# Attention and a feed-forward block on one core: weight loads moved to ScalarE's queue, the value scale taken through DRAM, the first batch's wide jobs moved behind the first hidden layer, half of a weight's low parts moved to VectorE

## The chip, the cores and the metric

The kernel runs on one core of a Trainium2 chip. The metric is the time of one execution in microseconds (us), the median of the runs taken. The core has a matrix engine (TensorE, PE in the profile, its weight loads PEld), VectorE (DVE), ScalarE (ACT), GpSimd (POOL) and SyncE (SP). Each runs its own instructions in a fixed order. DMAs are issued by SP and by ACT, in the order in which they stand among that engine's instructions; an engine that must wait before it issues a DMA keeps everything behind it waiting too. All DMAs are carried by the same 16 DMA engines.

## The reference

```python
# attention: batch 8, heads 8, 576 positions, head size 64; q, k, v, s are float32
scores = scale * np.matmul(q, k.transpose(0, 1, 3, 2))
cum = np.cumsum(np.maximum(s, 0.0), axis=-1)
bias = -(cum[:, :, :, None] - cum[:, :, None, :])
scores = np.where(causal, -1000000000.0, scores + np.minimum(bias, 0.0))
attn = softmax(scores)                       # row maximum taken off, eps 1e-9 in the sum
x = (attn @ v) as 4608 tokens x 512
# feed-forward: w_in 512 x 2048 and w_out 2048 x 512 are float64
h = x @ w_in
g = np.where(h >= 1, h, np.where(h <= -1, 0.0, (h + 1) ** 2 / 4))
out = (g @ w_out).astype(np.float32)
```

## The kernel before

Every product of the feed-forward block is made of three 16-bit products: each operand is split into a high and a low half (both float16), and high x high, low x high and high x low are added in PSUM. So weights, `x` and `g` are all held as pairs of halves.

**Weights.** `w_in` (w1 in the code) and `w_out` (w2) arrive as 64-bit numbers in 16 chunks each, 512 KB a chunk. `Weights.load` (L190) loads one into a raw buffer; there are four raw buffers for each weight, so that a later load waits until an earlier chunk has been read out. `decode` rebuilds float32 from the two words: a copy on ACT (L199), a shift on DVE (L200), one more ACT pass for every second chunk (L212), one or two combining passes on DVE (L213, or L215 and L216), and a matmul with ones (L204) that sums a group for its bound. `scale` turns a group's sums into a power-of-two factor (w1 has four groups, w2 two). `split` then makes the halves: the high one on ACT (L229); the low one either on DVE in one instruction (L237) or, for the chunks in the table `POOL_LO`, on POOL (L235), which for w2 needs one more ACT pass first (L234). w2's loads begin only when `a_in`, the largest bound of w1, is known (L623, L185), and so do the scales that every hidden activation needs.

**Attention** goes through 64 jobs: a batch has four head pairs, each with a narrow half (the first 320 queries, three query tiles) and a wide half (the last 256 queries over all 576 keys, two tiles). All four narrow jobs of a batch come first, then its four wide ones. A job loads q and k (L328 for the first eight jobs, L344 later), makes scores (L411; later L416 and L417), takes mask and row minimum on DVE (L422), exponentials on ACT (L433), row sums and their reciprocal on DVE (L449, L450), splits the weights into halves `pb` on POOL and DVE (L454 to L460), transposes them by DMA into `pt` (L461), multiplies by the transposed values `vt` (L479) and leaves `x` (L490, L491). `att_slot` deals a job out in eight slots.

**Value scale.** For each batch the largest magnitude of v over all 128 partitions is needed in every partition (`msc`, in `batch_scales_v`). `column_max` turns the column of 128 maxima into a row by a PE transpose (L97) and takes its maximum on DVE (L99); `spread` converts it (L105), multiplies it by ones on PE (L107) and copies the resulting column out of PSUM (L108).

**Feed-forward.** `ffn_h` makes one of 16 tiles of the hidden layer from `x` (12 matmuls, L534), ACT and DVE turn it into g (L546, L549, L550), ACT and POOL split it (L560, L561). `ffn_y` multiplies g by w2 (L573). Each batch has a narrow and a wide half here too.

**What sets the order.** The program is written as one stream, and a scheduler puts each instruction in its engine's order by priority and by an estimate of time; `tc.high_priority` moves what it encloses ahead. At the start the stream holds the first narrow jobs beside the 16 chunks of w1. Then a loop over `j` begins: in the first 16 steps it holds the hidden layer of the first narrow half, in the next 16 the products with w2 of that half; beside them stand w2's decoding and splitting (`w2_tasks`, two tasks a step, so 16 steps) and slots of attention, 40 in these 32 steps:

```python
for _ in range(1 + (j % 4 == 3 if j < 2 * NFT else j % 8 == 3 and j < 6 * NFT)):
    att_slot(t // 8, t % 8)
    t += 1
```

SP's queue carries s, q, k, v, all weight chunks, the transposes by DMA and the cumulated sums; ACT's carries outputs and two small loads a job.

## Time and profile before

| | |
|---|---|
| median of 3 runs | 1113.92 us (1113.88 to 1118.03) |
| the profiled execution's own time | 1117.59 us |
| span of its profile | 1115.8 us |
| busy: PE, PEld | 1013.1 us (91%), 777.3 us (70%) |
| busy: DVE, ACT, POOL | 843.6 us (76%), 731.0 us (66%), 637.1 us (57%) |
| DMA packets | 340925, 155.09 MB |
| transfers on SP's queue (q1), on ACT's (q10) | 143.68 MB, 9.84 MB |

The span runs from the first to the last instruction of the program; the execution's own time holds a little more, 1.8 us here. Busy time is an average over stages: in the profile's 40 slices PE is at 3 to 8 tenths in the first seven and at 8 or 9 from then on, so the start of the program and its long middle have to be read apart.

### The profile page before, as it was taken

To read this page: it belongs to the slowest core of one execution; us is meant where nothing else is said; L and a number is where in the kernel's file an instruction comes from. 1 tells how busy PE (TensorE), PEld (TensorE's weight loads), DVE (VectorE), ACT (ScalarE), POOL (GpSimd) and SP (SyncE) were. 2 spreads that over 40 slices of the span, in tenths; PEclk is the share of its full clock that TensorE was granted. 3 is DMA by queue.
4 is the path that set the end of the run, shared out by engine and by line. 5 is a ranking of instruction groups with operands and counts; after the bars stand their busy time and mean duration, and the time that the engine had idled before them with its cause. 6 is when DMAs were issued, how large, how long until landed. Compare 5 with 4: busy or idle time off the path is not lost.

```text
span 1115.8 us, 24709 instructions
## 1 busy us (share of the span) xinstructions
PE 1013.1 (91%) x8495; PEld 777.3 (70%) x8496; DVE 843.6 (76%) x2327; ACT 731.0 (66%) x1711; POOL 637.1 (57%) x846
## 2 busy tenths in 40 slices
PE   3558788899999999899999999899988999999998
PEld 1224456687777877787777877687767877787787
DVE  6877895787777877787877887787777888887533
ACT  4856787677576765777576765677576756776432
POOL 3555667666456664566566655556467665666422
PEclk9967889899999999999999999999999999999999
DMA  6986864776387663878377764668379663776300
GB/s 222 213 190 178 177 143 103 157 153 153 83 166 164 150 139 84 190 156 152 83 160 163 147 136 84 169 147 165 68 159 181 145 145 80 162 155 126 67 25 20
DMA packets 340925, 155.09 MB, mean 139 GB/s; under 512 B 290984, under 2 KB 322572, under 8 KB 340800
## 3 DMA queue, kind: packets, MB, share of 16 engines
q1 hardware_dynamic: 331200, 143.68, 60.2%
q10 hardware_dynamic: 9600, 9.84, 2.7%
q8 instruction: 67, 1.10, 0.4%
q14 instruction: 58, 0.48, 0.1%
HBM read 72.28 MB, written 9.88 MB: 74 GB/s over the span
## 4 chain that ended last, share of the span: by engine, by line
PE 58%; DMA 12%; DVE 11%; POOL 8%; issue 6%; ACT 4%; SPq 1%; ACTq 0%; DVEq 0%; POOLq 0%
PE h L534 25%; PE y L573 23%; DMA pt<-pb 5%; PE px L479 4%; PE s L416 3%; PE s L417 3%; DMA wir<-in_moe_w_in_dram 2%; POOL pb L457 2%; POOL pb L454 2%; DMA vt<-vb 2%; DVE pb L460 2%; DVE PS L422 1%; POOL g L561 1%; DMA wor<-in_moe_w_out_dram 1%; DVE h L549 1%
## 5 line engine op out<-in xcount | busy, mean ns | idle before, releaser
L534 PE MATMUL h<-x,WI 128*128 128x256 f16 (+1 forms) x3072 | 462.8, 292 | 8.0 <-DVE u L550 6.2
L573 PE MATMUL y<-g,WO 128*128 128x256 f16 (+1 forms) x3072 | 451.0, 288 | 9.7 <-POOL g L561 7.3
L534 PEld LDWEIGHTS <-WI 128*128 128x128 f16 x3072 | 290.3, 100 | 106.0 <-issue 21.4
L573 PEld LDWEIGHTS <-WO 128*128 128x128 f16 x3072 | 287.8, 98 | 97.0 <-issue 18.6
L561 POOL TENSOR_TENSOR g<-u,g 128x320 f16<-128x320 f32 (+1 forms) x256 | 208.6, 815 | 175.8 <-ACT g L560 175.5
L433 ACT ACTIVATE PS<-PS,mn 64x64 f32<-64x64 f32 (+4 forms) x320 | 178.8, 559 | 131.4 <-DVE mn L422 114.3
L546 ACT ACTIVATE u<-h,ub,us 128x320 f32<-128x320 f32 (+1 forms) x256 | 148.8, 582 | 116.1 <-PE h L534 100.9
L454 POOL TENSOR_SCALAR pb<-PS,rs 64x128 f16<-64x128 f32 (+4 forms) x160 | 101.0, 631 | 207.1 <-DVE rs L450 136.1
L549 DVE SCALAR_TENSOR_TENSOR h<-h,ws,u 128x320 f32<-128x320 f32 (+1 forms) x256 | 132.3, 518 | 107.8 <-ACT u L546 106.5
L457 POOL TENSOR_TENSOR pb<-PS,pb 64x128 f16<-64x128 f32 (+4 forms) x160 | 168.0, 1050 | 11.5
L460 DVE SCALAR_TENSOR_TENSOR pb<-PS,rs,pb 64x128 f16<-64x128 f32 (+4 forms) x160 | 135.1, 845 | 49.6 <-POOL pb L454 49.0
L422 DVE CUSTOM_DVE_ANT_0 PS<-s,mask 64x64 f32<-64x64 f32 (+4 forms) x320 | 133.3, 419 | 26.3 <-PE s L417 23.4
L550 DVE SCALAR_TENSOR_TENSOR u<-u,r,h 128x320 f32<-128x320 f32 (+1 forms) x256 | 130.0, 508 | 6.6
L416 PE MATMUL s<-K,Q 128*64 128x64 f32 (+1 forms) x336 | 126.3, 378 | 6.2 <-DVE mn L422 2.6
L455 ACT ACTIVATE PS<-PS,rs 64x64 f32<-64x64 f32 (+4 forms) x160 | 88.9, 559 | 49.2 <-DVE rs L450 49.1
L560 ACT CAST g<-u 128x320 f16<-128x320 f32 (+1 forms) x256 | 107.9, 422 | 13.5 <-DVE u L550 13.4
L417 PE MATMUL s<-K,Q 68*64 68x64 f32 (+1 forms) x336 | 102.8, 309 | 7.2 <-POOL K L367 4.3
L479 PEld LDWEIGHTS <-vt 128*64 128x64 f16 x1536 | 73.5, 114 | 49.2 <-issue 37.2
L479 PE MATMUL px<-pt,vt 128*64 128x256 f16 (+3 forms) x1536 | 83.4, 259 | 23.7 <-DMA pt<-pb 20.9
L456 POOL TENSOR_SCALAR pb<-PS 64x128 f16<-64x128 f32 (+4 forms) x160 | 90.5, 566 | 21.0 <-ACT PS L455 19.0
L416 PEld LDWEIGHTS s<-K,Q 128*64 128x64 f32 (+1 forms) x336 | 61.5, 183 | 17.1 <-DVE mn L422 3.2
L417 PEld LDWEIGHTS s<-K,Q 68*64 68x64 f32 (+1 forms) x336 | 61.9, 185 | 9.5 <-POOL K L367 4.4
(108 smaller groups left out, 930.3 us busy)
## 6 DMA issues: line engine op xcount, KB each, us to landing
rk<-in_k_dram SPq DMA_DIRECT2D x56, 288.0 KB
v<-in_v_dram SPq DMA_DIRECT2D x32, 288.0 KB
rq<-in_q_dram SPq DMA_DIRECT2D x56, 160.0 KB
rk<-in_k_dram SPq DMA_DIRECT2D x56, 160.0 KB
wir<-in_moe_w_in_dram SPq DMA_DIRECT2D x16, 512.0 KB
wor<-in_moe_w_out_dram SPq DMA_DIRECT2D x16, 512.0 KB
rq<-in_q_dram SPq DMA_DIRECT2D x56, 128.0 KB
out_dram<-o ACTq DMA_DIRECT2D x32, 160.0 KB
```

The source lines that it names most:

```text
L416: T.matmul(sc[:R, :c1 - c0], Q1[:, hd, qo:qo + R], K1[:, hd, c0:c1], start=True, stop=False)
L417: T.matmul(sc[:R, :c1 - c0], Q2[:KC, hd, qo:qo + R], K2[:KC, hd, c0:c1], start=False, stop=True)
L422: ttr[0] = V.tensor_tensor_reduce(out=Pt[:R, c0:c1], in0=sc[:R, :c1 - c0], in1=mask[:R, mo:mo + c1 - c0], scale=-0.125 if j < F32_JOBS els ...
L433: A.activation(Pt[:R, :W], Pt[:R, :W], AF.Exp, bias=m2[:R], scale=-1.0, accum_out=sums[n, i][:R, hd:hd + 1])
L457: G.tensor_tensor(los[1], pw, his[1], ALU.subtract)
L460: V.scalar_tensor_tensor(los[0], pv, rs[:R, :1], his[0], ALU.mult, ALU.subtract)
L479: T.matmul(px[hd * D:(hd + 1) * D, lo:N], VT[:, vl * NB + j, hd * D:(hd + 1) * D], PT[:, 4 * j + 2 * hd + pl, lo:], start=(m == 0), stop=( ...
L534: T.matmul(h[:, :N], WI[4 * kt + ft // 4][:, wl, ft % 4 * P:(ft % 4 + 1) * P], x[:, kt, xl], start=(n == 0), stop=(n == 3 * NKT - 1),)
L546: first = A.activation(u, h[:, :N], AF.Relu, bias=ubi[b], scale=usc[b][:, fg:fg + 1]).ins
L549: V.scalar_tensor_tensor(h[:, :N], h[:, :N], wsc[b][:, fg:fg + 1], u, ALU.mult, ALU.max)
L561: G.tensor_tensor(g[:, 1], u, g[:, 0], ALU.subtract)
L573: T.matmul(ys[b, hf, m][:, :N], WO[8 * (m // 2) + ft // 2][:, wl, c0:c0 + P], g[:, gl], start=(ft == 0 and n == 0), stop=(ft == NFT - 1 an ...
```

## The change

Five things change.

1. The chunks of both weights are issued by ACT (`WQ = nc.scalar`) in place of SP. The first three loads stand ahead of the first q and k in the program, and s, the cumulated sum, these three loads and the first job's q and k are given a higher priority.
2. The value scale goes through DRAM: the column of 128 maxima is written to a DRAM tensor `md`, read back broadcast to all partitions as `ma` (both DMAs on SP), and DVE takes the maximum of 128 numbers in each partition. `column_max`, `spread` and the identity matrix with its two POOL instructions go.
3. The 40 slots of attention that stood beside the first 32 steps all stand in the second 16 steps (two and three a step).
4. `POOL_LO['wo']` holds every second chunk in place of all: eight of w2's low halves are made on DVE by one instruction each, and their eight extra ACT passes go.
5. Some memsets at the start stand in another order.

```diff
-POOL_LO = {'wi': (8, 12, 13, 14, 15), 'wo': range(16)}
+POOL_LO = {'wi': (8, 12, 13, 14, 15), 'wo': range(0, 16, 2)}
...
-    LOADQ, CUMQ = nc.sync, nc.scalar
+    LOADQ, CUMQ, WQ = nc.sync, nc.scalar, nc.scalar
...
-    def column_max(src, name):
-
-        row = ps_s.tile([P, 512], F32, tag="s", name=f"row_{name}")
-        T.transpose(row[:1, :P], src, ident)
-        top = ap.tile([P, 1], F32, tag="top", name=f"top_{name}")
-        V.tensor_reduce(top[:1], row[:1, :P], axis=AX, op=ALU.max)
-        return top[:1]
-
-    def spread(dst, top, name):
-
-        t16 = ap.tile([P, 1], BF16, tag="t16", name=f"t16_{name}")
-        V.tensor_copy(t16[:1], top)
-        col = ps_s.tile([P, 512], F32, tag="s", name=f"col_{name}")
-        T.matmul(col[:, :1], ones[:1], t16[:1], start=True, stop=True)
-        V.tensor_copy(dst, col[:, :1])
...
+    with tc.high_priority(offset=2 * START_LEAD):
+        nc.sync.dma_start(st[:BH], s)
+        V.memset(QF[0][D:KF32], 8.0)
...
+        V.tensor_scalar(st[:BH], st[:BH], 0.0, None, ALU.max)
+        V.tensor_tensor_scan(cum[:BH], st[:BH], zr, 0.0, ALU.add, ALU.add)
...
-    ident = cp.tile([P, P], F32, name="ident")
-    G.memset(ident, 0.0)
-    G.affine_select(
-        out=ident, in_=ident, pattern=[[-1, P]], compare_op=ALU.not_equal,
-        fill=1.0, base=0, channel_multiplier=1,
-    )
...
-                nc.sync.dma_start(dst, src)
+                WQ.dma_start(dst, src)
...
+        d = dp.tile([P], F32, name=f"md{b}")
+        nc.sync.dma_start(d.rearrange("(p o) -> p o", o=1), t)
+        a = ap.tile([P, P], F32, tag="ma", bufs=1, name=f"ma{b}")
+        nc.sync.dma_start(a, d.partition_broadcast(P))
         m = msc[b] = ap.tile([P, 1], F32, tag="mb", name=f"mb{b}")
-        spread(m, column_max(t, f"m{b}"), f"m{b}")
+        V.tensor_reduce(m, a, axis=AX, op=ALU.max)
...
-    att_load(0, 0)
-    for c in range(3):
-        w1.load(c)
+    with tc.high_priority(offset=2 * START_LEAD):
+        for c in range(3):
+            w1.load(c)
+        att_load(0, 0)
...
-        for _ in range(1 + (j % 4 == 3 if j < 2 * NFT else j % 8 == 3 and j < 6 * NFT)):
+        if j < NFT:
+            slots = 0
+        elif j < 2 * NFT:
+            slots = 2 + j % 2
+        else:
+            slots = 1 + (j % 8 == 3 and j < 6 * NFT)
+        for _ in range(slots):
             att_slot(t // 8, t % 8)
             t += 1
```

Line numbers of the changed kernel are 17 to 21 lower than those of before for the same statement (L199 is L178, L490 is L473). Three places show what the scheduler made of the change.

The first is ACT's order around the `x` of the last narrow job of the first batch (`px_0_690`, before `px_0_699`). `wir` is a raw chunk of w1, `wor` one of w2, `L199` the copy that decoding begins with. Before:

```order
L199 ACTIVATE WO_141<-wir_579 128x512
L229 ACTIVATE WI_113<-WO_129,r_wi 128x512
L229 ACTIVATE WI_117<-WO_133,r_wi 128x512
L229 ACTIVATE WI_121<-WO_137,r_wi 128x512
L229 ACTIVATE WI_125<-WO_141,r_wi 128x512
L199 ACTIVATE WO_128<-wor_740 128x512
L490 ACTIVATE x_0_440<-px_0_699,ex_297 128x320
```

And in the changed kernel, where a row `L169 DMA` is a load of a chunk that ACT now issues:

```order
L169 DMA wor_815<-in_moe_w_out_dram 128x2x512
L178 ACTIVATE WO_127<-wor_790 128x512
L191 ACTIVATE wor_790<-wor_790,floor_bias 128x512
L178 ACTIVATE WO_128<-wor_815 128x512
L169 DMA wor_822<-in_moe_w_out_dram 128x2x512
L169 DMA wor_848<-in_moe_w_out_dram 128x2x512
L178 ACTIVATE WO_129<-wor_822 128x512
L169 DMA wor_855<-in_moe_w_out_dram 128x2x512
L191 ACTIVATE wor_822<-wor_822,floor_bias 128x512
L169 DMA wor_881<-in_moe_w_out_dram 128x2x512
L178 ACTIVATE WO_130<-wor_848 128x512
L473 ACTIVATE x_0_431<-px_0_690,ex_288 128x320
```

Before, the copy of one chunk of w2 stands ahead of this `x`; now eight do, four of them above the rows shown, and ten of w2's sixteen loads.

The second is POOL's order where w2's low halves (L235, now L214) stand among the second halves of g (L561, now L544). Before, from the end of the first half-batch's hidden layer on:

```order
L561 TENSOR_TENSOR g_0_12_1330<-u_0_15_1432,g_0_12_1330 128x320
L379 TENSOR_SCALAR vb_1769<-v_0_1054,rc_1629 128x576
L457 TENSOR_TENSOR pb_3_1590<-PS_151,pb_3_1590 128x4x128
L235 TENSOR_TENSOR WO_134<-WO_136,WO_134 128x512
L235 TENSOR_TENSOR WO_135<-WO_137,WO_135 128x512
L235 TENSOR_TENSOR WO_136<-WO_138,WO_136 128x512
L235 TENSOR_TENSOR WO_137<-WO_139,WO_137 128x512
L235 TENSOR_TENSOR WO_138<-WO_140,WO_138 128x512
L235 TENSOR_TENSOR WO_139<-WO_141,WO_139 128x512
L367 TENSOR_TENSOR K_107<-rk_0_1599,K_1749 64x2x320
```

And now the last four of POOL's eight:

```order
L214 TENSOR_TENSOR WO_129<-WO_131,WO_129 128x512
L544 TENSOR_TENSOR g_0_8_1041<-u_0_8_1042,g_0_8_1041 128x320
L214 TENSOR_TENSOR WO_131<-WO_133,WO_131 128x512
L544 TENSOR_TENSOR g_0_8_1041<-u_0_9_1075,g_0_8_1041 128x320
L214 TENSOR_TENSOR WO_133<-WO_135,WO_133 128x512
L544 TENSOR_TENSOR g_0_8_1041<-u_0_10_1106,g_0_8_1041 128x320
L214 TENSOR_TENSOR WO_135<-WO_137,WO_135 128x512
L544 TENSOR_TENSOR g_0_8_1041<-u_0_11_1135,g_0_8_1041 128x320
```

The low halves end four tiles of g before the hidden layer does, where before eight of them stood behind its last tile (two more follow the K_107 row).

The third is DVE's order at the value scale of the third batch: from the column of maxima (`mt`) to the scale in every partition (`mb`). Before:

```order
L274 TENSOR_REDUCE mt_3403<-c_3393 128x1
L550 SCALAR_TENSOR_TENSOR u_0_10_3599<-u_0_10_3599,r_2411,h_0_10_3586 128x320
L270 TENSOR_SCALAR rc_3394<-rc_3394 128x4
L549 SCALAR_TENSOR_TENSOR h_0_11_3643<-h_0_11_3643,ws_2421,u_0_11_3656 128x320
L99 TENSOR_REDUCE top_m_3408<-row_m_3406 1x1
L550 SCALAR_TENSOR_TENSOR u_0_11_3656<-u_0_11_3656,r_2411,h_0_11_3643 128x320
L105 CAST t_m_3410<-top_m_3408 1x1
L549 SCALAR_TENSOR_TENSOR h_0_12_3730<-h_0_12_3730,ws_2421,u_0_12_3744 128x320
L550 SCALAR_TENSOR_TENSOR u_0_12_3744<-u_0_12_3744,r_2411,h_0_12_3730 128x320
L108 COPY mb_3405<-col_m_3412 128x1
```

And now:

```order
L253 TENSOR_REDUCE mt_3382<-c_3372 128x1
L432 TENSOR_SCALAR rs_4_3438<-sm_4_3339 128x2
L533 SCALAR_TENSOR_TENSOR u_0_10_3574<-u_0_10_3574,r_2390,h_0_10_3561 128x320
L249 TENSOR_SCALAR rc_3373<-rc_3373 128x4
L433 RECIPROCAL rs_4_3438<-rs_4_3438 128x2
L474 SCALAR_TENSOR_TENSOR x_1_3012<-px_1_3445,ex_1687,x_1_3012 128x256
L405 ISA PS_144,mn_0_0_0_3523<-s_0_0_0_3520,mask 64x64
L405 ISA mn_0_0_0_3523 64x1
L443 SCALAR_TENSOR_TENSOR pb_4_3437<-PS_148,rs_4_3438,pb_4_3437 128x5x128
L532 SCALAR_TENSOR_TENSOR h_0_11_3618<-h_0_11_3618,ws_2400,u_0_11_3631 128x320
L259 TENSOR_REDUCE mb_3388<-ma_3386 128x1
```

Nine instructions stand between `mt` and the reduction that waits for the broadcast `ma`, where before eight stood between, two of them (L99, L105) part of the hop itself.

More of the change, by code (lines that the diff above doesn't have):

```diff
@@ L119, in attention_ffn @@
     st = ap.tile([P, S], F32, tag="vraw", bufs=4, name="st")
-    nc.sync.dma_start(st[:BH], s)
     ch = ap.tile([P, 2, S], F32R, tag="raw", name="ch")
-    zr = ch[:BH, 1].bitcast(F32)
-    V.memset(zr, 0.0)
-    V.memset(QF[0][D:KF32], 8.0)
-    V.memset(KF[0][D:KF32], -8.0)
-    V.tensor_scalar(st[:BH], st[:BH], 0.0, None, ALU.max)
     cum = ap.tile([P, S], F32, tag="raw", name="cum")
-    V.tensor_tensor_scan(cum[:BH], st[:BH], zr, 0.0, ALU.add, ALU.add)
     cumf = dp.tile([BH, S], F32, name="cumf")
     cumd = dp.tile([BH, 2, S], F32, name="cumd")
+    with tc.high_priority(offset=2 * START_LEAD):
+        nc.sync.dma_start(st[:BH], s)
+        V.memset(QF[0][D:KF32], 8.0)
+        zr = ch[:BH, 1].bitcast(F32)
+        V.memset(zr, 0.0)
+        V.memset(KF[0][D:KF32], -8.0)
+        V.tensor_scalar(st[:BH], st[:BH], 0.0, None, ALU.max)
+        V.tensor_tensor_scan(cum[:BH], st[:BH], zr, 0.0, ALU.add, ALU.add)
     mask = cp.tile([P, S], F32, name="mask")
```

## The prediction

> **What bounds the kernel now.** First the busy time of the engines by stage. A row of this view gives a stretch, its length, then busy us (and instructions) of PE, PEld, DVE, ACT and POOL, the clock granted to PE, the share of time in which the 16 DMA engines were busy, and GB/s.
>
> ```profile
> 0.00:90.00 90.00, 41.40 (x158) 21.47 (x159) 66.33 (x198) 54.48 (x114) 46.23 (x70) 0.84 0.81 211
> 90.00:195.00 105.00, 89.55 (x579) 57.94 (x580) 82.34 (x212) 79.21 (x154) 66.18 (x66) 0.89 0.62 144
> 205.00:1060.00 855.00, 826.29 (x7285) 650.48 (x7284) 671.33 (x1865) 573.81 (x1389) 506.19 (x685) 0.99 0.65 138
> ...
> 30.00:90.00 60.00, 30.87 (x132) 16.91 (x132) 45.11 (x140) 39.07 (x88) 34.77 (x46) 0.76 0.88 208
> ```
>
> From 205 us on PE is busy 826.29 of 855 us (97%) at a clock of 0.99. The change takes almost no PE work away, so the long middle can give little. What is left is the start, where PE stands for 49 of the first 90 us and 15 of the next 105. The two stretches are cut where ACT writes the `x` that lets the next layer begin:
>
> ```profile
> 89.20 0.66 ACT L199 ACTIVATE WO<-wor 128x512 f32<-128x512 f32 x1 [3.39 <-DMA wor<-in_moe_w_out_dram]
> 89.77 0.51 ACT L490 ACTIVATE x<-px,ex 128x320 f16<-128x320 f32 x1
> ...
> 194.74 0.47 ACT L490 ACTIVATE x<-px,ex 128x256 f16<-128x256 f32 x1 [1.64 <-PE px L479]
> ...
> 86.52 1.65 PE L479 MATMUL px<-pt,vt 128*64 128x320 f16 x18 [7.41 <-DMA pt<-pb]
> ```
>
> Stage 1 ends with the last narrow `x` at 90 us, stage 2 with the last wide `x` at 195, and from there both kernels have the same work left. In stage 1 `px` was done at 88.2, but `x` stood behind the copy of w2's first chunk, which landed at 89.2. So weights decide the end, by when they are loaded. The view of waits (waiting line, what ended it, us in total, times, longest) says who held them:
>
> ```profile
> ACT WO L199 <- DMA wir<-in_moe_w_in_dram: 18.0, 7, 7.2
> ACT WO L199 <- DMA wor<-in_moe_w_out_dram: 8.8, 6, 3.4
> ...
> SPq L461 <- DVE pb L460: 21.9, 10, 7.8
> SPq L461 <- POOL WO L235: 16.3, 3, 6.7
> ```
>
> ACT waits 26.8 us for chunks, while SP, which issues them, stands in front of transposes that wait for DVE and POOL. One chunk shows it, by DVE's and SP's order of time (start, us, instruction):
>
> ```profile
> 60.52 1.38 DVE L216 SCALAR_TENSOR_TENSOR WO<-wir,WO 128x512 int32<-128x512 int32 x1
> ...
> 62.73 3.41 SPq L392 DMA_TRANSPOSE vt<-vb  x1
> 68.50 1.40 SPq L461 DMA_TRANSPOSE pt<-pb  x1
> ...
> 71.76 0.38 SPq L190 DMA_DIRECT2D wir<-in_moe_w_in_dram  x1
> ...
> 4.12 1.54 SPq L190 DMA_DIRECT2D wir<-in_moe_w_in_dram  x3
> ...
> 13.62 2.50 SPq L190 DMA_DIRECT2D wir<-in_moe_w_in_dram  x3
> ```
>
> w1's last chunk could be loaded at 61.9, when DVE had read the buffer out (60.52 + 1.38), and was issued at 71.8: held 9.9 us. The fourth chunk has a buffer from the start, yet follows the first three (4.12 + 1.54) by 8.0 us, behind v and the sums. Both are on one path, since with four buffers every fourth chunk waits for the one before.
>
> **The change, part by part. Stage 1.** With loads on ACT these 17.9 us can go, and `a_in` with w2's first load, issued at 84.7 in the chain quoted below, comes at about 67. What is late next is not w1. As ACT's order shows, the last narrow `x` now stands behind the copy of w2's eighth chunk. Its time, from both sides:
>
> ```profile
> 84.68 4.44 DMA wor<-in_moe_w_out_dram
> ...
> 106.42 4.12 DMA wor<-in_moe_w_out_dram
> ...
> 110.61 5.70 SPq L190 DMA_DIRECT2D wor<-in_moe_w_out_dram  x3
> ```
>
> At the old pace the eighth load came 25.9 us after the first (84.68 to 110.61) and took some 4.1 to land: 67 + 30 = 97. From the other side the DMA engines: by 90 us they were busy 0.81 x 90 = 73 us; a chunk of 0.52 MB costs 0.52 / (211 / 0.81) = 2.0 us at their full rate, and five to seven chunks more must have landed, so 83 to 87 us of transfers, at the share of 0.88 that 30 to 90 us reached 94 to 99, and at a full share 83 to 87. DVE has to do seven more decodings:
>
> ```profile
> L200 DVE TENSOR_SCALAR WO<-WO 128x512 int32<-128x512 int32 x16 | 9.5, 591 | 5.6 <-ACT WO L199 5.6
> L216 DVE SCALAR_TENSOR_TENSOR WO<-wor,WO 128x512 int32<-128x512 int32 x8 | 7.0, 880 | 0.0
> L213 DVE SCALAR_TENSOR_TENSOR WO<-wor,WO 128x512 int32<-128x512 int32 x8 | 6.8, 850 | 1.6 <-ACT wor L212 1.6
> L215 DVE SCALAR_TENSOR_TENSOR WO<-wor,WO 128x512 int32<-128x512 int32 x8 | 6.1, 759 | 0.0
> ```
>
> These are all 16 chunks of w2: 29.4 us, 1.84 each, so 12.9 more on 66.3, which is 79 of 90 us. I take 92 for the end of stage 1 (84 to 99): the work that came in fills what the early loads free, and the gain is not an earlier `x` but that half of w2 is ready by then. The removed identity (its POOL instructions) and the reordered memsets I cost at nothing: they stand at the start, beside the first loads, before any score exists.
>
> **Stage 2.** Out of it go the seven decodings, 12.9 us of DVE. The low halves cost and save:
>
> ```profile
> L235 POOL TENSOR_TENSOR WO<-WO,WO 128x512 f16<-128x512 f32 x16 | 19.3, 1207 | 5.4 <-issue 2.6 <-ACT WO L234 2.6 <-POOL WO L235 0.3
> L234 ACT ACTIVATE WO<-WO,r_wo 128x512 f32<-128x512 f32 x16 | 11.3, 718 | 0.1
> ...
> L237 DVE SCALAR_TENSOR_TENSOR WI<-WO,r_wi,WI 128x512 f16<-128x512 f32 x11 | 8.9, 844 | 0.0
> ```
>
> Eight times 0.844 puts 6.8 us on DVE and takes 9.7 off POOL and 5.7 off ACT. DVE keeps 82.3 - 12.9 + 6.8 = 76.2 us. At its present pace of 0.784 (82.34 of 105) that is 97 us. The other bound is PE: 89.55 busy at a clock of 0.89 is 79.7 at full clock, and the order asks the same of it. Between them I look at what stands at the end of this stage, in the chain of work (start, us, what):
>
> ```profile
> 162.24 0.72 POOL WO L235
> 170.49 1.16 POOL WO L235
> 171.68 0.73 ACT WO L229
> 172.43 0.72 ACT WO L234
> ```
>
> Here w2's second split, eight chunks on ACT and POOL in turn, is the path, and a wide job's exponentials stand behind it. By the changed orders the split is over before the hidden layer is, so this piece, 11 us from the first row to the end of the last, becomes work beside h. That speaks for a time nearer to PE's bound than the old pace; against it, the 20 slots of attention that stood beside the hidden layer now stand behind it in the program, and the wide jobs still follow one another. I take 92, of 82 to 100.
>
> **The loads on ACT** cost its sequencer one issue each, 32 in all (SP's took 0.38 for the last of w1), beside arithmetic of ACT that runs on; ACT was busy 133.7 of the 195 us, so I cost them at nothing inside these stages. What they cost if ACT stands is a rival below.
>
> **The middle.** Seven batches lose two PE instructions and gain two DMAs that follow each other:
>
> ```profile
> L97 PE MATMUL row_m<-ident,mt 128*1 128x128 f32 x8 | 2.3, 285 | 1.0 <-DVE rc L270 1.0
> L107 PE MATMUL col_m<-t_m,ones 1*128 1x1 bf16 x8 | 1.4, 173 | 0.0
> L108 DVE COPY mb<-col_m 128x1 f32<-128x1 f32 x8 | 1.2, 152 | 7.1 <-PE col_m L107 7.1
> ...
> 296.60 0.12 DVE L274 TENSOR_REDUCE mt<-c 128x1 f32<-128x4 f32 x1
> 303.16 0.15 DVE L108 COPY mb<-col_m 128x1 f32<-128x1 f32 x1
> ...
> 12.44 0.50 SPq L156 DMA_DIRECT2D cumf<-cum  x1
> 16.80 0.68 SPq L336 DMA_DIRECT2D QF<-cumf  x1
> 2.18 3.23 DMA st<-in_s_dram
> ```
>
> PE saves at most 7 x (0.285 + 0.173) = 3.2 us. The new hop is a write to DRAM and a read that must wait for it. The nearest pair is cumf, written at 12.44 and read from 16.80, 4.4 us; a read like that of s lands 3.2 us after its issue. So up to 7.6 us and 0.6 for an issue, where the old hop took 6.6 (296.60 to 303.16). DVE, which waits for it in order with the g chain behind it, would stand at most 1.6 us longer a batch, 11 in seven, and no longer at all if the transfers are quicker than these two, which ran among big loads. I take 0 for the middle (-3 to +11). The Trainium skill's page DMA: Bandwidth & Descriptors (Latency and other measured facts) gives a DMA a fixed cost of about 2 us; by an estimate from it the pair would take 4 and DVE would wait less than before, and no run here shows such a pair.
>
> **Sum.** Stages: 92 + 92 = 184 in place of 195, so -11; the middle 0. The profiled execution's 1117.59 us (span 1115.8) would be 1106.6; the runs' median of 1113.92 becomes 1103.
>
> **Rivals.** *Given back (1114).* Stage 1 ends at 97, as the old pace of w2's loads has it, and stage 2 keeps DVE's pace: 97 + 97 = 194. For it: DMA and DVE are near 0.88 from 30 us on. Against it: SP's holds, which are not transfers. The Trainium skill's page DMA: Bandwidth & Descriptors (Issuing engines are not separate DMA queues) says that issuing from several engines saves only the sequencer's time to initiate a DMA, and by it this rival's time would come out; the trace disagrees, as the two holds above are waits in one engine's order and not issues. *Hop too slow (1114):* 1103 + 11. *Nearer PE (1087):* stage 1 at 86, since ten chunks need not all press at once, and stage 2 at 82, so -27. *Slower (1128): ACT stands before its loads.* 28 of 32 loads wait until DVE has read a buffer, and the exponentials behind them in ACT's order wait too. From 0.4 us exposed a load (11 / 28) the gain is gone; at 0.9, two thirds of the 1.38 us pass above, it costs 25 us. For it: every load's place in ACT's order is fixed by an estimate of when DVE is done. Against it: ACT was idle 61 us of the 195.
>
> **How the numbers follow.** Forecast 0.48 (0.04 of it within 0.5%), nearer PE 0.16, given back 0.16, hop too slow 0.07, slower 0.13. About 0.5%, 5.6 us, is what a measurement can tell from no change: faster 0.60, same 0.27, slower 0.13. The range leaves out the slower case and the last of the fastest: 1088 to 1119.
>
> **What would show it.** SP no longer stands before any weight; w1's last chunk is issued before 58 us and `a_in` stands before 70. The last narrow `x` is written at 86 to 97, right behind a copy of w2 that waited for its landing. The last wide `x` comes near 184, with no run of L235's successor behind the last g. In the middle PE stays near 97% and DVE's wait at `mb` under 2 us a batch. The forecast is wrong if ACT's waits before loads add up to over 11 us ahead of exponentials, or if DVE passes 0.9 of stage 2 while PE stands.

## The result, and the profile after

The changed kernel takes 1181.8 us (median of 4 runs, 1181.1 to 1187.5) against 1114.3 for the kernel before: a ratio of 1.061, 95% interval [1.058, 1.064]. It is slower by 68 us. The forecast was 1103, with 1088 to 1119 as its range, so size and sign were both wrong.

First the busy time by stage, cut at the same times as before (columns as there: PE, PEld, DVE, ACT, POOL, granted clock, DMA share, GB/s).

```profile
0.00:90.00 90.00, 33.80 (x113) 18.20 (x114) 62.77 (x191) 53.30 (x111) 37.48 (x57) 0.89 0.90 190
90.00:195.00 105.00, 79.81 (x469) 47.63 (x469) 73.27 (x156) 67.14 (x120) 53.46 (x54) 0.78 0.56 133
205.00:1060.00 855.00, 783.34 (x6838) 615.36 (x6836) 637.60 (x1823) 552.66 (x1348) 485.22 (x668) 0.96 0.65 136
```

Then ACT's order of time at the `x` of the last narrow and of the last wide job of the first batch.

```profile
115.64 0.66 ACT L178 ACTIVATE WO<-wor 128x512 f32<-128x512 f32 x1 [3.46 <-DMA wor<-in_moe_w_out_dram]
117.62 0.53 ACT L473 ACTIVATE x<-px,ex 128x320 f16<-128x320 f32 x1 [1.32 <-PE px L462]
...
230.00 0.46 ACT L473 ACTIVATE x<-px,ex 128x256 f16<-128x256 f32 x1
```

Every engine is less busy in the first 90 us, while the DMA engines are busier (0.90 for 0.81) and move less (190 GB/s for 211). The last narrow `x` comes at 117.6 (89.8 before), the last wide one at 230.0 (194.7), so stage 1 (up to the first of these) lost 27.8 us and stage 2 (from there to the second) 7.4. And the middle, which was to change by nothing, is longer too: from 230.0 to the end of the span at 1179.8 are 949.8 us, 921.1 before. PE fell from 826 to 783 busy us in the same 855. Who waits, and for what, by the view of waits over the whole run (us in total, times, longest):

```profile
DVE mb L259 <- DMA ma<-md: 60.4, 8, 8.9
...
ACT WO L178 <- DMA wir<-in_moe_w_in_dram: 19.2, 9, 7.7
ACT WO L178 <- DMA wor<-in_moe_w_out_dram: 19.1, 9, 4.2
```

DVE stands at the value scale in each of eight batches, 4.2 us in the first and 8.0 on average in the seven later ones. One batch, by SP's order and by DVE's:

```profile
205.40 0.35 SPq L255 DMA_DIRECT2D md<-mt  x1
213.46 0.34 SPq L257 DMA_DIRECT2D ma<-md  x1
213.90 0.61 SPq L327 DMA_DIRECT2D rq<-in_q_dram  x1
...
217.74 0.29 DVE L259 TENSOR_REDUCE mb<-ma 128x1 f32<-128x128 f32 x1 [8.95 <-DMA ma<-md]
```

The write of 512 bytes is issued at 205.4, and only at 213.5 may SP issue the read: 8.1 us, and 4.3 more until DVE goes on. The DMA view of two pieces of that wait shows that for most of it no packet is moving:

```profile
DMA packets 509, 0.34 MB, mean 190 GB/s; under 512 B 253, under 2 KB 509, under 8 KB 509
...
DMA packets 0, 0.00 MB, mean 0 GB/s; under 512 B 0, under 2 KB 0, under 8 KB 0
```

The first row is 205.5 to 207.3 us, the second 207.3 to 213.4. The pieces of 4 bytes have all left by 207.3, then for 6.1 us not one packet moves on the core, and SP still waits for the write's completion. The semaphore events of the trace show that wait at work: sixteen completions of the write arrive one after the other from 208.7 to 213.4 us, and the read goes out behind the last.

### The profile page after: what moved, and what is told of

It reads as the page before. It is cut to its first block, busy times and chain, and to the rows that moved or that the text cites. A ratio compares the mean times of both kernels' runs of the same rounds, so it can differ in the third digit from the quotient of the medians.

```text
span 1179.8 us, 24667 instructions
## 1 busy us (share of the span) xinstructions
PE 1021.5 (87%) x8480; PEld 779.9 (66%) x8480; DVE 839.5 (71%) x2319; ACT 730.5 (62%) x1703; POOL 625.4 (53%) x836
## 4 chain that ended last, share of the span: by engine, by line
PE 50%; DMA 20%; DVE 14%; issue 5%; POOL 5%; ACT 4%; SPq 1%; ACTq 0%; DVEq 0%; POOLq 0%
PE h L517 21%; PE y L556 20%; DMA md<-mt 6%; DMA vt<-vb 5%; PE px L462 4%; DMA ma<-md 3%; DMA pt<-pb 3%; PE s L399 3%; PE s L400 2%; POOL pb L437 2%; DVE PS L405 2%; DVE pb L443 2%; DVE Q L347 1%; DVE c L246 1%; ACT u L529 1%
## 5 line engine op out<-in xcount | busy, mean ns | idle before, releaser
L517 PE MATMUL h<-x,WI 128*128 128x256 f16 (+1 forms) x3072 | 467.8, 295 | 20.0 <-DVE u L533 13.9
L544 POOL TENSOR_TENSOR g<-u,g 128x320 f16<-128x320 f32 (+1 forms) x256 | 208.2, 813 | 199.0 <-ACT g L543 156.9
L437 POOL TENSOR_SCALAR pb<-PS,rs 64x128 f16<-64x128 f32 (+4 forms) x160 | 105.9, 662 | 249.7 <-DVE rs L433 175.3
L532 DVE SCALAR_TENSOR_TENSOR h<-h,ws,u 128x320 f32<-128x320 f32 (+1 forms) x256 | 133.0, 520 | 103.3 <-ACT u L529 103.0
L399 PE MATMUL s<-K,Q 128*64 128x64 f32 (+1 forms) x336 | 130.3, 389 | 39.4 <-DVE mn L405 25.8
L399 PEld LDWEIGHTS s<-K,Q 128*64 128x64 f32 (+1 forms) x336 | 63.3, 188 | 57.8 <-DVE mn L405 34.2
L439 POOL TENSOR_SCALAR pb<-PS 64x128 f16<-64x128 f32 (+4 forms) x160 | 86.8, 542 | 7.5 <-ACT PS L438 4.1
```

The source lines that it names most:

```text
L399: T.matmul(sc[:R, :c1 - c0], Q1[:, hd, qo:qo + R], K1[:, hd, c0:c1], start=True, stop=False)
L517: T.matmul(h[:, :N], WI[4 * kt + ft // 4][:, wl, ft % 4 * P:(ft % 4 + 1) * P], x[:, kt, xl], start=(n == 0), stop=(n == 3 * NKT - 1),)
L532: V.scalar_tensor_tensor(h[:, :N], h[:, :N], wsc[b][:, fg:fg + 1], u, ALU.mult, ALU.max)
L544: G.tensor_tensor(g[:, 1], u, g[:, 0], ALU.subtract)
```

## The experiments

For each kernel I read three numbers from its profiled execution: the last narrow `x`, the last wide `x`, and what lies behind it up to the end of the span. Ratios are to the kernel before on the same chip, with 95% intervals. The three numbers are of one execution each, while the runs of one kernel spread (the kernel before from 1107.9 to 1121.2 us in 16 runs), so a difference of a few us in them is no finding by itself. This table is worked out from the profiles and runs; the text goes through it.

```
kernel                                   last narrow x  last wide x  behind it  us, median  ratio
before                                            89.8        194.7      921.1      1114.3
changed                                          117.6        230.0      949.8      1181.8  1.061 [1.058, 1.064]
changed, PE's scale           (pe_scale)         103.0        209.7      917.5      1129.3  1.013 [1.008, 1.018]
changed, loads on SP        (sync_loads)          91.6        205.7      955.3      1164.2  1.042 [1.039, 1.045]
changed, both                  (pe_sync)          82.5        194.2      919.3      1117.5  1.003 [1.000, 1.005]
changed, old slots           (old_slots)         113.3        217.7      962.1      1181.4  1.057 [1.055, 1.060]
before + hop                  (hop_only)          83.0        189.4      964.2      1160.2  1.038 [1.035, 1.041]
before + loads on ACT         (act_only)          97.4        203.5      917.5      1123.7  1.008 [1.005, 1.011]
before + halves on DVE         (lo_only)          88.2        188.6      921.0      1111.9  0.999 [0.997, 1.001]
before + hop, reduce later    (hop_late)          82.0        188.2      941.3      1129.0  1.013 [1.008, 1.017]
before + hop, read later too (hop_split)          86.1        190.6      931.0      1126.1  1.011 [1.008, 1.015]
before + hop as one row        (hop_row)          85.4        198.9      917.7      1118.0  1.003 [1.000, 1.005]
changed, hop as one row      (row_after)         114.1        216.1      909.9      1127.1  1.012 [1.009, 1.015]
changed, row, loads on SP     (row_sync)          80.3        192.2      911.3      1104.1  0.991 [0.987, 0.994]
```

**Which part costs what.** Four kernels each undo or isolate one part.

```diff
-        nc.sync.dma_start(a, d.partition_broadcast(P))
...
-        V.tensor_reduce(m, a, axis=AX, op=ALU.max)
+        spread(m, column_max(t, f"m{b}"), f"m{b}")
```

> The changed kernel with the value scale computed by PE again (identity, transpose, one matmul), all else as changed. Theory A, the hop: DVE stands in order at mb for a write and a read through DRAM, 7 to 9 us a batch. Then the part behind the last wide x, 949.8 us in the changed kernel and 921.1 before, goes back to 918 to 925, and the whole comes to 1138 to 1153 us, the lower end if the hop also cost the first batch 15 us. Theory B, the loads on ACT's queue slow the whole start and the middle is slow for another reason: 1175 or more.

The part behind the last wide `x` came back to 917.5, the whole to 1129.3: theory A, the whole even below its range, and 52 of the 68 us are the hop's. 20 of them lie ahead of the last wide `x`.

```diff
-    LOADQ, CUMQ, WQ = nc.sync, nc.scalar, nc.scalar
+    LOADQ, CUMQ, WQ = nc.sync, nc.scalar, nc.sync
```

> The changed kernel with the weight chunks issued by SP again, all else as changed. Theory B, the start is late because chunks on a second queue share the DMA engines with the transposes and because ACT stands before its loads: the last narrow x goes from 117.6 back to 90 to 97 us and the whole to 1154 to 1162. Theory A, the hop in the first batch (mb at 48.0 us instead of 25.6) is what makes the start late: the last narrow x stays at 110 or later and the whole at 1174 to 1190. The part behind the last wide x stays near 950 by both.

The last narrow `x` went back to 91.6 as B has it, but the whole only to 1164.2, a little over B's range: ACT's queue costs the start, beside the hop.

The other way round, the change's lines for the hop in the kernel before:

```diff
+        d = dp.tile([P], F32, name=f"md{b}")
+        nc.sync.dma_start(d.rearrange("(p o) -> p o", o=1), t)
...
+        nc.sync.dma_start(a, d.partition_broadcast(P))
...
-        spread(m, column_max(t, f"m{b}"), f"m{b}")
+        V.tensor_reduce(m, a, axis=AX, op=ALU.max)
```

> The kernel before with the value scale through DRAM and nothing else. Theory A: the part behind the last wide x grows from 921 to about 950, and the first batch pays for its own hop too, 5 to 15 us: 1148 to 1158. Rival: the hop is costly only beside the other edits, then under 1125.

The hop by itself, added to the kernel before, costs 43.8 us (1160.2 against 1116.3 in the same runs), more than theory A said, all of it behind the last wide `x`; the last wide `x` itself came 5 us earlier in the execution that was profiled.

```diff
-        if j < NFT:
-            slots = 0
...
+        for _ in range(1 + (j % 4 == 3 if j < 2 * NFT else j % 8 == 3 and j < 6 * NFT)):
```

> The changed kernel with the slots of attention in the first batch as before (some beside h, some beside y), all else as changed. Theory C, the slots moved beside y make stage 2 longer (112.4 us against 104.9): 1172 to 1176. If the slots carry nothing of the loss: 1179 to 1186, and if they gain, 1187 to 1195.

1181.4: in the whole the slots carry nothing of the loss. In the profiled execution stage 2 is 8 us shorter with them back, and what lies behind it 12 us longer.

**What in the hop costs so much.** DVE stands at `mb`, and SP stands between the two transfers. Two kernels move the reduction one job of attention later, so that DVE has other work:

```diff
+        mas[b] = a
...
+    def batch_scales_m(b):
...
+            if k == M_K and jobs[j][0] % NPAIR == 0 and jobs[j][1] == 0 and j:
+                with tc.issue_after(ttr[0]):
+                    batch_scales_m(jobs[j][0] // NPAIR)
```

> The changed kernel with the second half of the value scale (the reduction of what came back from DRAM, and what follows it) written one job of attention later, so that DVE has other work while the hop is under way; the hop itself and SP's wait between its two transfers stay. Theory A1, DVE's standing is the price: the part behind the last wide x goes from 949.8 to 915 to 925, mt to mb becomes longer than 15 us and DVE's wait at mb falls under 1 us a batch; with a start like that of the kernel with PE's scale the whole comes to 1128 to 1142. Theory A2, SP's standing between the two transfers is the price (transposes and q/k loads queue behind it): the part behind the last wide x stays at 940 or above, the whole at 1160 to 1180.

> The kernel before with the value scale through DRAM, its second half written one job of attention later. Theory A1: the early start of the kernel with the hop alone (last wide x at 189.4) stays and the part behind it comes back to 915 to 925, so 1104 to 1116. Theory A2, SP's standing costs as much as DVE's: 1130 to 1155.

Neither theory alone. On the changed kernel the part behind the last wide `x` fell from 949.8 to 928.2 and the whole to 1162.1 (1.042 [1.037, 1.048]); its last wide `x` stayed late, at 233.3. `mt` to `mb` did not become longer, and DVE still stood 1.7 us a batch, so that expectation was wrong in both details. On the kernel before it fell from 964.2 to 941.3, and the whole from 1160.2 to 1129.0, a ratio of 1.013 in place of 1.038: DVE's standing is more than half of the loss, some 23 to 31 us. In that kernel SP still waits between write and read (view of waits, DVE's over the whole run, SP's from 240 to 1060 us):

```profile
DVE mb L288 <- DMA ma<-md: 12.8, 8, 3.2
...
SPq L280 <- DMA md<-mt: 31.2, 6, 6.1
```

So next the read was held back as well, until SP has other transfers to issue:

```diff
+    def batch_scales_a(b):
+        a = mas[b] = ap.tile([P, P], F32, tag="ma", bufs=1, name=f"ma{b}")
+        V.memset(a[:, :1], 0.0)
+        nc.sync.dma_start(a, mds.pop(b).partition_broadcast(P))
```

> The kernel before with the value scale through DRAM, its read back held on SP until four slots of attention into the next job (by a small store of DVE into its target) and its reduction three slots after that, so that neither SP nor DVE meets the hop while it is under way. Theory A3, the hop costs what stands behind it in order, about half on DVE (964.2 to 941.3 us behind the last wide x when only the reduction moved) and half on SP: the part behind the last wide x comes back to 916 to 924, the whole to 1102 to 1112. Rival, the transfers themselves disturb the others, or their store and read cost something wherever they stand: 935 or more, 1122 to 1132.

> The changed kernel with the chunks on SP's queue and with the hop taken apart as in the kernel before with the split hop; order at the start, slots beside y and the halves on DVE stay. By A3 its difference to the kernel with PE's scale and chunks on SP (1117.5, no change against before) is that of the other pair: the part behind the last wide x 916 to 924, the whole 1104 to 1118. Rival: 1125 or more.

931.0 and 933.4 behind the last wide `x`, 1126.1 and 1131.9 in all (the second 1.016 [1.012, 1.020]). What SP's standing costs can't be told: the profiled executions differ by 10 us behind the last wide `x` (941.3 and 931.0), but the runs by 3, with ratios of 1.013 [1.008, 1.017] and 1.011 [1.008, 1.015]. Some 10 us remain although the engines hardly meet the hop any more (in the first of the two kernels DVE waits 3.6 us in all at `mb`, SP in one batch 5.4 us for the write). So the rival holds: the transfers cost something wherever they stand. The packets' records show one way. In the changed kernel the write is followed on SP's queue by loads of q and k, 512 packets of 1280 bytes. Around the third later batch they take from 453.35 to 462.35 us, with single packets of up to 3.9 us; before, the same 512 packets went from 433.58 to 437.47, none over 0.40 us. In the kernel with the split hop three batches show 4.4, 7.0 and 6.1 us for the longest packet. So what stood behind the write on the same queue went slowly until the write was done.

What makes the write so slow? Its 512 bytes are 128 pieces of 4 bytes, one from each partition. One kernel turns the column into a row first, by the PE transpose of the kernel before, and writes it as one piece (the edit is shown against the kernel with the hop alone):

```diff
+        T.transpose(row[:1, :P], t, ident)
...
+        V.tensor_copy(tr[:1], row[:1, :P])
...
-        nc.sync.dma_start(d.rearrange("(p o) -> p o", o=1), t)
+        nc.sync.dma_start(d, tr[:1])
```

> The kernel before with the value scale through DRAM, but turned into one row by PE first, so that the write is one piece of 512 bytes from one partition in place of 128 pieces of 4 bytes; the read back and DVE's place are those of the kernel with the hop alone (1160.2 us). Theory W1, the 128 small pieces make the write slow (6 to 8 us from issue to the read's issue): now 2 to 4 us, and the whole 1130 to 1148. Theory W2, a write to DRAM that a read waits for takes this long whatever its pieces: 6 to 8 us again, the whole 1155 to 1170.

The same batch in the two kernels, by DVE's and SP's order of time, first the kernel with the hop alone:

```profile
426.40 0.12 DVE L274 TENSOR_REDUCE mt<-c 128x1 f32<-128x4 f32 x1
426.92 0.60 SPq L276 DMA_DIRECT2D md<-mt  x1
434.87 0.33 SPq L278 DMA_DIRECT2D ma<-md  x1
438.95 0.28 DVE L280 TENSOR_REDUCE mb<-ma 128x1 f32<-128x128 f32 x1 [8.52 <-DMA ma<-md]
```

Then the kernel with the row:

```profile
422.84 0.15 DVE L274 TENSOR_REDUCE mt<-c 128x1 f32<-128x4 f32 x1
425.93 0.25 SPq L280 DMA_DIRECT2D md<-tr  x1
427.03 0.36 SPq L282 DMA_DIRECT2D ma<-md  x1
429.91 0.28 DVE L284 TENSOR_REDUCE mb<-ma 128x1 f32<-128x128 f32 x1 [3.18 <-DMA ma<-md]
```

From the write's issue to the read's it is 1.1 us in place of 7.95, from the read to `mb` 2.9 in place of 4.1. W1 holds and more: the whole is 1118.0, below the range that W1 gave and within 0.5% of before (1.003 [1.000, 1.005]). So DVE's standing and the remaining 10 us both come from the form of one write of 512 bytes. (The row differs in three things that were not tried apart: the size of the pieces, the one partition that they come from, and the completions that the read waits for, two by the semaphore events, the last 1.08 us after the issue, in place of sixteen.) The Trainium skill's page DMA: Bandwidth & Descriptors (Specifications) says that below 512 bytes a DMA reads, modifies and writes what it stores to; the runs agree in that the pieces of 4 bytes are the slow ones, and the page gives no time for it. In the changed kernel the same edit gives:

> The changed kernel with one edit: the value scale goes to DRAM as one row of 512 bytes (turned by PE first) in place of 128 pieces of 4 bytes. If the shape of the write is the price of the hop: mt to mb 6 to 7 us, the part behind the last wide x 949.8 back to 915 to 922, the last wide x from 230 to 205 to 215, the whole 1122 to 1138, as with PE's scale (1129.3). If the hop hurts the start in another way, too (its two transfers on SP among the first transposes): the last wide x stays at 220 or later, the whole 1140 to 1155.

1127.1, as with PE's scale: the form of the write is the whole price of the hop there too. Its last narrow `x` stays late, at 114.1.

**What loads on ACT cost.** The hop taken out, SP's queue against ACT's:

> The changed kernel with PE's value scale and with the weight chunks on SP's queue: what is left of the change is the order at the start, the slots beside y and the halves of w2 on DVE. Theory B, the loads on ACT are the rest of the loss (13 us in the kernel with PE's scale, all of it ahead of the last narrow x): the last narrow x comes at 88 to 94 us and the whole at 1108 to 1118. Rival: order, slots or halves carry the loss: 1124 to 1132.

And ACT's queue in the kernel before:

```diff
-    LOADQ, CUMQ = nc.sync, nc.scalar
+    LOADQ, CUMQ, WQ = nc.sync, nc.scalar, nc.scalar
...
-                nc.sync.dma_start(dst, src)
+                WQ.dma_start(dst, src)
```

> The kernel before with the weight chunks issued by ACT and nothing else. Theory B: w1's last chunk is issued before 58 us, yet the first x comes some 10 us later and the last narrow x at 98 to 104 us: 1124 to 1131. Rival, the loads on ACT are harmless by themselves: the last narrow x at 85 to 92, 1105 to 1117.

With PE's scale and SP's queue the last narrow `x` comes at 82.5, earlier than before, and the whole is no different from before. With ACT's queue and nothing else changed the kernel before is 0.8% slower. That is 12 and 8 us for the loads on ACT, a little less than B had it in the second case, although it does what the forecast said: in `pe_scale` w1's last chunk is issued at 47.1 us and `a_in` stands at 65.4.

```profile
65.36 0.14 DVE L625 TENSOR_REDUCE a_in<-bound_wi 128x1 f32<-128x4 f32 x1
...
103.00 0.53 ACT L491 ACTIVATE x<-px,ex 128x320 f16<-128x320 f32 x1 [1.27 <-PE px L480]
```

The weights came 17 us earlier and the last narrow `x` 13 us later. Two theories: weights now run ahead of attention (B1), or two queues on the same DMA engines slow each other (B2).

```diff
-    for c in range(3):
+    for c in range(2):
...
-                w1.load(c + 3)
+                w1.load(c + 2)
```

> The changed kernel with PE's value scale (1129.3 us), its weight chunks on ACT but w1's with one chunk less under way (two ahead in place of three). Theory B1, chunks that come early push decoding and their sums ahead of the first jobs of attention in the orders of DVE and PE: the first x comes from 61.5 back to 45 to 54 us, the last narrow x from 103.0 to 85 to 95, the whole 1112 to 1122. Theory B2, a second queue beside the transposes slows both whatever is under way: last narrow x 100 to 108, the whole 1127 to 1135.

1132.2 (1.016 [1.014, 1.018]), last narrow `x` at 106.8, as B2 said; but w1's last load was issued at 47.2, as without the edit, so this run moved no load and tells nothing. The next ties each load to the scores of attention, then issues the same gated loads from SP:

```diff
+        if R == P:
+            gate[0] = m2
...
-                w1.load(c + 3)
+                w1.load(c + 3, gate[0])
```

> The changed kernel with PE's value scale (1129.3 us), chunks on ACT, but each load of w1 from the seventh chunk on waits (by a store of one column on DVE) until the latest scores of attention have been reduced, so that weights no longer run ahead of attention. Theory B1, early chunks push their decoding and sums ahead of attention: the first x from 61.5 to 45 to 55 us, the last narrow x from 103 to 84 to 95, the whole 1110 to 1121. Theory B2, the second queue slows the transposes and the chunks, whenever they are issued: the last narrow x stays at 99 or later, the whole 1126 to 1140.

> The kernel with gated loads of w1 (1138.1 us) with one edit: the chunks are issued by SP. Theory B2, the second queue beside the transposes is what costs: the last narrow x from 107.4 back to 82 to 94 us, the whole 1110 to 1122, and no transpose takes over 8 us to land. Rival, the gates cost it: the last narrow x at 100 or later, the whole 1128 to 1140.

Gated on ACT's queue: 1138.1 (1.021 [1.018, 1.025]), the last narrow `x` at 107.4, though w1's last chunk is issued at 72.9, as late as before. Gated on SP's queue: 1122.0 (1.009 [1.006, 1.012]), the last narrow `x` at 84.5. So 16 us lie between two kernels that differ in one word of the program. They do not differ in the queue alone: the scheduler orders by an estimate of time, and with the queue every engine's order changes, DVE's from its eighth instruction on. So B1 does not fall with the late loads. This table, worked out from the traces, has the five pairs of kernels that differ in the queue, SP's first and ACT's second: the last narrow `x`; the copies of w1's chunks that stand ahead of the first narrow `x` in ACT's order; those of w2's chunks ahead of the last one; DVE's time on weights ahead of its own half of that `x`, in DVE's order; and the mean time of the transposes' packets up to that `x`.

```
                     last narrow x   w1 copies   w2 copies   DVE on weights, us   packet, ns
before               89.8    97.4     11   15      1    7        35.8   51.4      22.1   24.0
changed, PE's scale  82.5   103.0     10   16      0    8        36.8   47.1      23.3   21.5
the same, gated      84.5   107.4      9   12      0    4        35.0   39.2      25.5   28.9
changed              91.6   117.6      9   14      0    8        38.7   45.7      22.2   29.7
changed, row         80.3   114.1      9   15      0    9        35.0   53.1      25.6   26.1
```

In every pair ACT's queue comes with more of the weights' work ahead of attention, 4 to 18 us of DVE's time (B1). In the first two pairs and the last the transposes' packets take the same time within 2 ns, and attention is late all the same; in the gated pair and in the changed kernel they are slower as well (B2). No run kept the order and changed the queue, so what each of the two costs is not shown.

What slow transfers look like is read from stretches of 10 us in which transposes and chunks are under way together, with the columns of the stages above. The gated kernel on SP's queue, then on ACT's:

```profile
30.00:40.00 10.00, 3.56 (x9) 1.69 (x11) 9.52 (x28) 8.44 (x20) 6.39 (x9) 1.00 0.99 234
```

```profile
40.00:50.00 10.00, 0.80 (x2) 0.10 (x1) 2.94 (x11) 1.22 (x4) 0.00 (x0) 1.00 1.17 120
```

The DMA share adds up the packets' times; over 1 it means that packets on one engine overlap, which happens on one queue too (1.12 at 282 GB/s in the gated kernel on SP's queue, 50 to 60 us). In these two stretches one queue moves 234 GB/s and two move 120, and DVE, ACT and POOL run dry meanwhile. In the packets' records of the second a transpose's packet takes 69 ns on average (28 in the first) and a chunk's 456 (220). What waits for it in that kernel:

```profile
POOL vb L378 <- DMA vt<-vb: 13.8, 1, 13.8
DVE WO L214 <- ACT wir L213: 10.3, 1, 10.3
ACT vb L382 <- DMA vt<-vb: 9.3, 1, 9.3
```

One transpose issued at 34.2 us landed at 51.4, and POOL, ACT and DVE behind ACT stood for it. Other stretches with both queues are not like this: the kernel with PE's scale moves 294 GB/s from 20 to 30 us and 281 from 40 to 50, the kernel before with loads on ACT 276 from 40 to 50. Which meeting of transposes and chunks is the bad one stays open.

**The other parts, and a faster kernel.** First the hop in the first batch alone:

```diff
+        if b:
...
+            spread(m, column_max(t, f"m{b}"), f"m{b}")
+        else:
...
+            nc.sync.dma_start(d.rearrange("(p o) -> p o", o=1), t)
```

> The kernel before with the value scale through DRAM in the first batch only; the seven others keep PE's. The kernel with the hop alone had its last wide x at 189.4 us (194.7 before). If that lead is the first batch's own: last wide x 187 to 191, the part behind it 917 to 922, the whole 1104 to 1110. If it was chance of the order: within 0.5% of 1114.

1116.2 (1.002 [1.000, 1.005]). The last narrow `x` came at 80.6, nine us ahead of before, and the last wide one at 194.1, as before: a lead in stage 1 is lost in stage 2.

```diff
-POOL_LO = {'wi': (8, 12, 13, 14, 15), 'wo': range(16)}
+POOL_LO = {'wi': (8, 12, 13, 14, 15), 'wo': range(0, 16, 2)}
```

> The kernel before with half of w2's low halves on VectorE and nothing else. By the forecast's rows it takes 9.7 us off POOL and 5.7 off ACT at the end of stage 2, where the split is the path, for 6.8 on DVE: the last wide x from 194.7 to 184 to 191, the whole 1104 to 1111. Rival: DVE, busy 82 of 105 us there, gives it back: within 0.4% of 1114.

1111.9, no difference that can be told, though the profiled execution has its last wide `x` 6 us earlier.

Last, the changed kernel with the row and with the chunks on SP's queue:

> The changed kernel with two edits: chunks on SP's queue, and the value scale written as one row of 512 bytes. If the two are the change's whole loss and the rest is worth what the part behind the last wide x showed with the row (909.9 us in place of 921.0): last wide x 190 to 200, the whole 1100 to 1110. If that part was chance of the order: 1112 to 1120, no difference from before.

1104.1, a ratio of 0.991 [0.987, 0.994]: 0.9% faster than the kernel before. That is the change without the pieces of 4 bytes and without the loads on ACT. Its rows by stage:

```profile
0.00:90.00 90.00, 49.02 (x174) 25.98 (x175) 70.10 (x207) 57.56 (x120) 41.51 (x67) 1.00 0.81 207
90.00:195.00 105.00, 85.08 (x571) 53.69 (x569) 91.77 (x212) 75.32 (x145) 67.46 (x67) 0.97 0.65 156
205.00:1060.00 855.00, 826.08 (x7328) 650.10 (x7326) 672.83 (x1857) 574.47 (x1391) 516.52 (x683) 1.00 0.66 138
```

PE is at 49 us in the first 90 (41 before, 34 in the changed kernel). Most of the gain lies behind the last wide `x`, 911.3 us for 921.1, and the kernel with the row and the loads on ACT has it too (909.9), while PE's scale with the same edits (919.3) and the row alone (917.7) have not. Why the gain needs the row and the other edits together is not settled.

## Why the prediction was wrong, point by point

1. *SP's holds go with loads on ACT, `a_in` comes at about 67.* The mechanism was right: without the hop `a_in` stands at 65.4 and w1's last chunk is issued at 47.1. In the changed kernel itself they are 78.0 and 60.7, since the first batch's hop took 12.0 us from write to read (31.7 to 43.7) and DVE stood for it.

2. *Stage 1 ends at 92 (84 to 99).* It ended at 117.6, at 103.0 without the hop, and at 82.5 with neither the hop nor ACT's queue. Two steps failed. The first is that the work that came in fills what the early loads free. DVE's total was sized right (79 us; 82.7 in the kernel with PE's scale), but not its place: there all 16 copies of w1 stand ahead of the first narrow `x`, 11 before, and that `x` comes at 61.5 (50.6 before). The second is the DMA engines' rate, 2.0 us a chunk from 0.52 / (211 / 0.81): it took the share for busy time that ends at 1 and one queue's rate for two. In the changed kernel both show in the chain of work (its longest pieces: start, us, what): a chunk of w2, its copy and sum, DVE's `pb` behind them, then a transpose that takes 9.8 us to land:

```profile
96.84 5.79 DMA wor<-in_moe_w_out_dram
102.64 0.67 ACT WO L178
103.88 0.60 PE sum_wo L183
104.73 1.20 DVE pb L443
105.98 9.83 DMA pt<-pb
```

The `x` did come right behind the copy of w2's eighth chunk (115.64, after 3.46 us of waiting), as the order showed, but `px` was no earlier.

3. *ACT's issues cost nothing.* The issues themselves do not: ACT's idle time ahead of its loads, up to the last narrow `x`, adds up to 8.2 us in the changed kernel and 4.0 in the one with PE's scale, under the 11 that the prediction set as the sign of the rival "ACT stands before its loads" (12.1 in the kernel before with loads on ACT, so there it is not excluded). In the changed kernel the rival had the right sign for another reason. (Its 28 loads that wait for a buffer are 24; three more wait for `a_in`.) What the loads on ACT cost is 8, 12, 16, 18 and 23 us in the five pairs (the kernel before, the changed one with PE's scale, gated, as it is, and with the row); with it go other orders in all of them and slower transfers in two, and which of the two costs how much stays open. The Trainium skill's page DMA: Bandwidth & Descriptors (Issuing engines are not separate DMA queues) says that several issuers only save a sequencer's time; the runs agree in that nothing was won by it; here the change of issuer lost time, in part by other orders.

4. *Stage 2 takes 92 (82 to 100).* 112.4 in the changed kernel, 106.7 with PE's scale, 111.7 with SP's queue too, 104.4 with the old slots. The point named against it, the slots moved behind the hidden layer, accounts for 8 of the 20 us that were missed. The changed kernel's stage 2, cut in pieces:

```profile
158.00:178.00 20.00, 20.00 (x144) 13.46 (x140) 13.48 (x29) 15.07 (x28) 12.60 (x13) 1.00 0.16 31
178.00:198.00 20.00, 20.00 (x151) 13.43 (x149) 9.61 (x26) 9.38 (x20) 9.09 (x10) 1.00 0.41 88
198.00:230.00 32.00, 17.35 (x139) 13.26 (x138) 19.06 (x67) 12.16 (x31) 13.93 (x18) 0.73 0.50 106
```

For 40 us PE is full while DVE is idle for 17, then for 32 us the wide jobs follow one another and PE is idle for 15; 9 us of that stretch are DVE's wait for the hop of the second batch. The failing step is the overlap: 92 lies between two bounds, PE's 80 and DVE's 97, that hold if the engines work side by side, and the new order lays a part of the work end to end. The halves on DVE, costed at a gain of 9.7 us on POOL, showed none in the whole.

5. *The middle: 0, at most 11 longer.* 28.7 longer, and 43 where the hop was alone. The failing step is the bound for the write: 4.4 us from `cumf`, 64 pieces of 2304 bytes, for a write in 128 pieces of 4. It took 6.6 to 8.5. The read was bounded at 3.2 us plus 0.6 and took 3.6 to 4.3, near enough. The second error was to count only DVE's wait: some 10 us remain when DVE and SP hardly meet the hop, and loads behind the write on SP's queue had packets of up to 7.0 us. The rival "hop too slow" named the mechanism and priced it at 11 us in place of 52 in the whole.

6. *What would show it.* PE was to stay near 97% in the middle; it fell to 92% (783 of 855). DVE's wait at `mb` was to be under 2 us a batch; it was 8.0. w1's last chunk and `a_in` were to come before 58 and 70 us; they came so only without the hop (47.1 and 65.4).

## What to carry to other kernels

A small write to DRAM that something waits for is priced by its pieces, not by its bytes: gather a column into a row before it goes to DRAM, and look at what stands behind the wait, on the engine that consumes and on the queue. Moving loads to a second queue freed the issuing engine here and won nothing: with the queue every engine's order changed, and in some stretches transposes and loads slowed each other. So before a loss is put down to a queue, the orders of the two kernels have to be compared, and then the GB/s in the stretch where both kinds of transfer run. And when a change has several parts, a forecast needs a bound for each from rows of the same form, and the runs may show, as here, that the parts without the two bad ones are worth keeping.

## What was not expected of the hardware

- A write of 128 pieces of 4 bytes from 128 partitions to DRAM took 6.4 to 9.1 us from its issue to the issue of the read that waited for it, in the seven later batches of the changed kernel and of the kernel with the hop alone, 6.1 us of it in the batch shown without one packet under way; the same 512 bytes in one piece from one partition took 1.1 to 1.9. Sixteen completions of the slow write arrived over 4.7 us in that batch.
- While such a write was under way, the longest packets of loads behind it on the same queue took 3.9 to 7.0 us, where 0.40 was the longest before.
- Transposes on SP's queue and loads of 512 KB on ACT's together moved 120 GB/s in one stretch of 10 us, where the same kernel with one queue moved 234 in a like stretch, and a transpose took 17 us to land; in other stretches both queues together moved 276 to 294.
